# MLP rows written straight to the output, segments' rows added there by DMA: one core of Trainium2, a recurrent attention kernel beside an MLP

## The chip, the cores and the metric

One core of a Trainium2 chip runs the whole kernel. Engines are named as in the profile: PE is TensorE (its weight loads are PEld), DVE is VectorE, ACT is ScalarE, POOL is GpSimd, SP is SyncE. SP and ACT issue DMAs on hardware queues, POOL on the software queue (q0 in the profile). The metric is the device time of one execution in microseconds (us), lower is better. In "the profiled execution" the same program ran under the hardware profiler.

## The reference, cut to what matters

```
xn  = layernorm(x)                                   # 2048 rows of 1024
out = x + A(xn) + B(xn)

B(xn) = gelu(xn @ w1 + b1) @ w2 + b2                 # F = 3584

A(xn): mem = mem0                                    # 8 rows
  for each of 64 segments of 32 rows xs:
      h = concat(mem, xs)                            # 40 rows
      q, k, v = h @ Wq, h @ Wk, h @ Wv               # 32 heads of 128
      p = softmax(mask(q @ k.T / sqrt(128)))
      o = (p @ v) @ Wo
      mem = o[:8]                                    # read by the next segment
      yield o[8:]
```

The segments depend on each other through `mem`; the MLP, B, does not depend on them. The kernel calls `x + B(xn)` of a row its residual, and the output of a row is its residual plus its row of A.

## The kernel before, in words

**First stage, the MLP (to about 417 us).** Rows are tiled by 128, four tiles to a group `tg`, four groups. Each group makes layer norm, transposes, the first product (L468), gelu and the second product (L589; in the last group L622, with b2 and x added by PE at L615 and L616). `keep_xT` writes the transposed rows to DRAM (`hr_d` by segments, `hrL_d` by groups of segments). `keep_R` (L418) writes the residual rows to the DRAM tile `R_n`; those of the last group are issued by ACT. `turn_R` (L455, L457) then copies them with small DMAs from `R_n` into the second halves of `hr_d` and `hrL_d`, in the layout in which the segments' results lie. SP issues these copies for groups 0 and 1, POOL those for group 2, and those of the last group go into a list, `small`, from which POOL issues one or two at each streamed unit in segments 1 to 4.

**Second stage, 64 segments in order.** The weights Wq, Wk, Wv and Wo are cut into 64 units of 512 KB. 46 are resident in SBUF: they are fetched into places that the MLP gives up (`fetch_resident`), and four of them, `LATE`, into a pool `late` that opens after the MLP's pools have closed. The other 18 are streamed in every segment through six slots (`start_stream`, L257 and L259): when PE has used a unit, `unit_done` gives its slot to the next one and SP issues the load. Two of the 18 are kept in PSUM banks and copied from there by DVE (L246). Of one unit of Wo, `PART`, 768 of 2048 columns stay in SBUF, in `half_home`, and the rest (320 KB) is streamed.

A segment's queries, keys and values are made of 24 of its 32 rows and the memory. The 8 rows left over by each of four segments ("left rows") are put together with those of the other three, and their products, made beside those of the segments, serve a group. The order in a segment is: K of the first half of the heads, Q, K of the second half, Q, V, V, then O (`O_UNITS`). In the second K/Q part stand the scores, the exponential `pr` (L860) into the tile `pr_all`, two minima that apply the mask (L867), the sums of the first half (`sums(0)`: products L875 and L881, a logarithm and exponentials on ACT at L886 and L889, DVE's products into `pd_main` and `pd_left` at L896 and L900). The second half follows in the V part, so `pr_all` and `pd_main` are written twice in every segment. `scores(0)` comes after K, Q and K, some 7 us into the segment.

The result of O stands in a PSUM tile `psX`. Three segments of four have their own rows alone in it, 128 partitions by 256 columns; DVE adds the folded half (L1084). The others (`left_o`, 16 of them and the last segment) have 128 by 512, with the left rows of up to four segments, and ACT copies them (L1081). From there PE and DVE put the memory rows into the next segment's transposed input (`put_mem`, L291 and L295). That is the step from segment to segment.

Then DVE adds the residual (L1104). The residual of an ordinary segment lies in `res_home`, half of the tile `hr_home`, and comes with the next x rows in one load of 128 KB (`load_x_rows`, L268; in the first segments two loads of 64 KB by ACT). That of the left rows is loaded into `pr_all` (L1072). POOL then stores the sum with four DMAs (L1137), or, with left rows, first to the DRAM tile `outL_d` (L1109) and from there to the output (L1134). In the last segment SP and ACT store it directly (L1126).

The tiles at the head of SBUF stand at written addresses. `SCRATCH`, 384 bytes of a partition, is for POOL's DMA descriptors, and behind it:

```python
    half_home = nc.alloc_sbuf_tensor_at("half_home", [P, DM], BF16, offset=SCRATCH)
    hr_home = nc.alloc_sbuf_tensor_at("hr_home", [P, 512], BF16, offset=SCRATCH + 2048)
    pd_main = nc.alloc_sbuf_tensor_at("pd_main", [P, 320], BF16, offset=SCRATCH + 3072)

    part_home, pr_all, res_home = half_home[:, 0:PART_COLS], half_home[:, PART_COLS:DM], hr_home[:, 256:512]
```

So in the profile of before `pr_all` appears as `half_home`, and the residual as `hr_home`. [...]

## Time and profile before

| | |
|---|---|
| three runs, us | 1840.64, 1843.55, 1832.82 (median 1840.64) |
| profiled execution, us | 1839.26 |
| its span (first to last instruction), us | 1837.5 |
| granted TensorE clock | 0.996 |
| busy, share of the span | PE 93%, PEld 49%, DVE 52%, ACT 36%, POOL 15% |
| DMA, whole span | 612.94 MB, mean 334 GB/s |
| MLP, segments | to about 417 us, from there to the end |

A busy PE is not PE at its peak: the ends of matmuls are modelled, and short gaps disappear. Waits are put down to the event that came last. Several lines below come from a view of one stretch or one engine in order of time. In a line of the timeline the numbers are start and length in us, and the square bracket tells how long the engine was idle before and what ended that. [...]

### The profile page before, as it was taken

The page shows a single profiled execution, that of the slowest core. Times are in us where ns is not written, and L with a number is a line of the kernel's source. Part 1 is how long each engine was busy: PE and PEld are TensorE (multiplying, and loading weights), DVE is VectorE, ACT ScalarE, POOL GpSimd, SP SyncE. Part 2 cuts the span into 40 slices and gives each one's busy share as a digit, 9 for nine tenths or more (in the row PEclk, how much of TensorE's full clock was granted, in tenths as well). Part 3 has the DMA queues.
Part 4 walks back from the last instruction along what each step waited for, and adds up shares of the span by engine and source line. Part 5 has one row for each costly group of instructions (what it writes and reads, how often), then busy time and mean ns, then how long its engine had stood idle before and what let it go on. Part 6 is the DMA issues. An engine that isn't in the chain of part 4 may idle for free.

```text
span 1837.5 us, 69927 instructions
## 1 busy us (share of the span) xinstructions
PE 1717.9 (93%) x30556; PEld 893.2 (49%) x30576; DVE 955.3 (52%) x2330; ACT 663.8 (36%) x1429; POOL 284.4 (15%) x559
## 2 busy tenths in 40 slices
PE   8999999998999999999999999999999999999997
PEld 4444444444454445454545545454545454545444
DVE  7657483805454545555454555455545454545543
ACT  6334251602333333333333333333333333333333
POOL 0000001501342111111111111112111111111111
PEclk9999999999999999999999999999999999999999
DMA  9931212769999999999999999999999999999998
GB/s 286 313 98 46 55 44 57 260 209 371 397 404 389 391 384 389 381 394 388 373 397 386 400 385 394 374 390 401 389 384 390 383 398 391 397 376 384 389 393 313
DMA packets 229278, 612.94 MB, mean 334 GB/s; under 512 B 46795, under 2 KB 76027, under 8 KB 228972
## 3 DMA queue, kind: packets, MB, share of 16 engines
q1 hardware_dynamic: 207252, 588.05, 84.3%
q0 software_dynamic: 17408, 17.69, 3.0%
q8 instruction: 239, 3.92, 0.8%
q10 hardware_dynamic: 4312, 2.73, 0.5%
q14 instruction: 67, 0.55, 0.1%
HBM read 594.40 MB, written 29.23 MB: 339 GB/s over the span
## 4 chain that ended last, share of the span: by engine, by line
PE 32%; DMA 18%; DVE 4%; ACT 2%; issue 1%; POOL 0%; DVEq 0%; ACTq 0%; SPq 0%
PE acc L739 22%; DMA u<-Wc_K 10%; PE acc L962 6%; DMA outL_d<-half_home 3%; DMA u<-Wc_O 3%; ACT mixed L889 1%; DVE b_oL L804 1%; PE acc L915 1%; DMA hr_home<-hr_d 1%; DVE pd_main L896 1%; PE mixed L848 1%; DMA u<-Wc_V 1%; ACT mixed L886 1%; DMA u<-Wc_Q 0%; PE mixed L854 0%
## 5 line engine op out<-in xcount | busy, mean ns | idle before, releaser
L739 PE MATMUL acc<-u,hr_home 128*32 128x512 bf16 x11520 | 770.8, 380 | 34.0 <-DMA u<-Wc_K 18.2
L739 PEld LDWEIGHTS <-hr_home 128*32 128x32 bf16 x12288 | 342.1, 96 | 317.3 <-issue 57.3
L739 PE MATMUL acc<-u,hrL 128*32 128x512 bf16 x2880 | 248.8, 379 | 3.0 <-DVE folded L978 3.0
L468 PE MATMUL ps<-u 128*128 128x512 bf16 (+1 forms) x920 | 195.7, 375 | 2.0 <-ACT u L388 2.0
L246 DVE TENSOR_SCALAR u<-kept 128x512 uint32<-128x512 uint32 x254 | 163.5, 685 | 35.4 <-PE acc L962 12.3
L962 PE MATMUL acc<-u,d_oL 128*32 128x512 bf16 (+1 forms) x1792 | 153.3, 381 | 11.7 <-DMA u<-Wc_O 9.4
L790 ACT CAST kT<-acc 128x512 bf16<-128x512 f32 x64 | 37.4, 585 | 307.6 <-PE acc L739 307.5
L589 PE MATMUL ps<-u 128*128 128x512 bf16 x657 | 146.2, 379 | 0.8
L962 PEld LDWEIGHTS <-b_oL 128*32 128x32 bf16 (+1 forms) x3381 | 108.4, 98 | 74.5 <-issue 35.9
L896 DVE TENSOR_TENSOR pd_main<-half_home,mixed 128x320 bf16<-128x320 bf16 x128 | 62.4, 487 | 153.2 <-ACT mixed L889 153.2
L468 PEld LDWEIGHTS <-u 128*128 128x128 bf16 x920 | 90.5, 99 | 105.5 <-issue 2.4
L1137 POOL DMA_DIRECT2D out_dram<-hr_home x188 | 96.3, 512 | 294.1 <-DVE hr_home L1104 280.5
L962 PE MATMUL acc<-u,b_oL 128*32 128x256 bf16 (+2 forms) x2062 | 117.1, 289 | 20.2 <-DMA u<-Wc_O 19.5
L804 DVE STREAM_TRANSPOSE b_oL<-b_oL 128x512 bf16<-128x512 bf16 x128 | 90.6, 708 | 64.8 <-ACT b_oL L790 64.8
L268 POOL DMA_DIRECT2D hr_home<-hr_d x58 | 32.8, 565 | 581.3 <-PE acc L739 576.1
L962 PEld LDWEIGHTS <-d_oL 128*32 128x32 bf16 (+1 forms) x2048 | 70.3, 99 | 84.7 <-issue 28.0
L739 PEld LDWEIGHTS <-hrL 128*32 128x32 bf16 x3072 | 82.9, 96 | 51.2 <-issue 7.7
L790 ACT CAST b_oL<-acc 128x512 bf16<-128x512 f32 x128 | 75.1, 587 | 86.1 <-PE acc L739 86.1
L589 PEld LDWEIGHTS <-u 128*128 128x128 bf16 x672 | 65.3, 98 | 77.3 <-DVE g_u L550 0.4
L889 ACT ACTIVATE mixed<-mixed,small_consts 128x160 f32<-128x160 f32 x256 | 94.2, 368 | 8.4
L542 ACT ACTIVATE g_xb<-ps,b1col 128x512 bf16<-128x512 f32 x112 | 76.8, 686 | 55.5 <-PE ps L468 54.7
L794 ACT CAST v<-acc 128x512 bf16<-128x512 f32 x128 | 75.1, 587 | 48.9 <-PE acc L739 48.6
(129 smaller groups left out, 2011.6 us busy)
## 6 DMA issues: line engine op xcount, KB each, us to landing
u<-Wc_K SPq DMA_DIRECT2D x320, 512.0 KB
u<-Wc_V SPq DMA_DIRECT2D x256, 512.0 KB
u<-Wc_O SPq DMA_DIRECT2D x256, 512.0 KB
u<-Wc_Q SPq DMA_DIRECT2D x128, 512.0 KB
u<-Wc_O SPq DMA_DIRECT2D x64, 320.0 KB
u<-in_B_w_dram SPq DMA_DIRECT2D x28, 512.0 KB
hr_home<-hr_d POOLq DMA_DIRECT2D x58, 128.0 KB, 5.5
u<-in_A_Wq_dram SPq DMA_DIRECT2D x14, 512.0 KB
```

The costliest lines, as they stand in the source:

```text
L246: nc.vector.tensor_single_scalar(out=out, in_=in_, scalar=0, op=ALU.bitwise_or)
L468: nc.tensor.matmul(ps[:, SEG * s0:SEG * s1].rearrange("p (s t) -> p s t", t=SEG), lhsT=w1_sb[fb // 2][:, kt, (fb % 2) * P:(fb % 2 + 1) * P ...
L542: nc.scalar.activation(out=xb[:, :], in_=ps[:, :], func=ACT.Identity, bias=b1col[:, fb:fb + 1], scale=1.0)
L589: nc.tensor.matmul(ps[:, :], lhsT=gts[fc // 4][:, fc % 4, t * P:(t + 1) * P], rhs=w2_sb[fc // 2][:, fc % 2, cs], start=(fc == 0), stop=(fc ...
L739: nc.tensor.matmul(o, lhsT=lhs[:, i, :], rhs=m, start=(i == seq[0]), stop=(i == seq[-1]), tile_position=(0, 32 * j),)
L790: cp(out=out, in_=ps.rearrange("p (h e) -> p h e", e=32))
L794: cp(out=t[:, :], in_=ps[:, :])
L804: nc.vector.transpose(out=home, in_=home)
L889: nc.scalar.activation(out=mixed[:, 160 * b:160 * b + 160], in_=mixed[:, 0:160], func=ACT.Exp, scale=-1.0, bias=off[:, b:b + 1],)
L896: nc.vector.tensor_tensor(out=pdA.rearrange("p c b q -> p b c q"), in0=prA[:, None, :, :].to_broadcast([P, 2, 4, 40]), in1=dd, op=ALU.mult,)
L962: nc.tensor.matmul(acc[r0:r0 + rows, c:c + wide], lhsT=lhs[:, 4 * (i % 4) + 2 * u + k, :], rhs=cols, start=start, stop=stop, tile_position ...
L1137: nc.gpsimd.dma_start(out=out_flat[rows, 256 * j:256 * j + 256], in_=res[32 * j:32 * j + NX, :])
```

## The change

`keep_R` writes the residual rows into the output itself. `R_n`, `outL_d`, `turn_R`, the list `small`, all loads of residuals and DVE's L1104 go. At the end of a segment the sum of A stands in `pr_all` (256 columns), with left rows also in `pd_main`; `put_mem` reads it there, and POOL issues DMAs that add it to the output's rows (`accum_op`): four for an ordinary segment, eight with left rows, in the last segment too. `hr_d` and `hrL_d` hold only x rows, so a load is 64 KB, and POOL issues it in all segments. `half_home` keeps 1024 columns of `PART`, and 256 KB of it are streamed; `pr_all` is a tile of its own, where half of `hr_home` was. The MLP's pool of small tiles `ma` is closed ahead of the last group's second product, and `late` is opened there with the four LATE units fetched at once; the first two places of the queue `late_units` are now those of `xt2` and `xt3`.

```diff
-    hr_d = dram.tile([NSEG + 1, P, 512], BF16, name="hr_d")
-    hrL_d = dram.tile([NGRP + 1, P, 512], BF16, name="hrL_d")
-    R_n = dram.tile([S, DM], BF16, name="R_n")
-    outL_d = dram.tile([NGRP, 2 * SEG, DM], BF16, name="outL_d")
+    hr_d = dram.tile([NSEG, P, 256], BF16, name="hr_d")
+    hrL_d = dram.tile([NGRP, P, 256], BF16, name="hrL_d")
...
-    hr_home = nc.alloc_sbuf_tensor_at("hr_home", [P, 512], BF16, offset=SCRATCH + 2048)
+    hr_home = nc.alloc_sbuf_tensor_at("hr_home", [P, 256], BF16, offset=SCRATCH + 2048)
+    pr_all = nc.alloc_sbuf_tensor_at("pr_all", [P, 256], BF16, offset=SCRATCH + 2560)
...
         elif unit == PART:
-            nc.sync.dma_start(out=t[:, PART_COLS:], in_=copies[unit])
+            nc.sync.dma_start(out=t[:, DM:], in_=copies[unit])
...
     def load_x_rows(s, eng=nc.sync):
-        n = 512 if s > 5 else 256
-        eng.dma_start(out=hr_home[:, 0:n], in_=hr_d[s, :, 0:n])
-        nxt["hT"] = hr_home[:, 0:256].rearrange("p (k t) -> p k t", k=KT)
+        eng.dma_start(out=hr_home[:, :], in_=hr_d[s, :, :])
+        nxt["hT"] = hr_home.rearrange("p (k t) -> p k t", k=KT)
...
             eng = nc.scalar if ttg >= NT - 4 else nc.sync
-            eng.dma_start(out=R_n[ttg * P:ttg * P + P, :], in_=rsb[:, :])
+            eng.dma_start(out=out_flat[ttg * P:ttg * P + P, :], in_=rsb[:, :])
...
-                for t in range(4):
-                    turn_R(4 * tg + t, nc.gpsimd if tg == 2 else nc.sync)
...
+                mlp.close()
+                late = ctx.enter_context(tc.tile_pool(name="late", bufs=1))
+                for unit in LATE:
+                    res_tiles[unit] = late.tile([P, 2048], BF16, name="W_" + "_".join(map(str, unit)))[:, :]
+                    fetch(res_tiles[unit], unit)
                 for fc in range(FC):
...
-        late_units = deque(lambda unit=unit: fetch_late(unit) for unit in LATE)
-        late_units += [lambda: fetch_resident("xt2"), lambda: fetch_resident("xt3")]
+        late_units = deque([lambda: fetch_resident("xt2"), lambda: fetch_resident("xt3")])
...
-            if 1 <= s <= 4:
-                turn_R(NT - 5 + s, nc.gpsimd, small)
...
-                load_x_rows(s + 1, nc.scalar if s < 5 else nc.gpsimd)
+                load_x_rows(s + 1, nc.gpsimd)
...
+            o_tiles = [pr_all[:, :], pd_main[:, 0:256]] if left_o else [pr_all[:, :]]
+            if left_o:
+                nc.scalar.copy(out=o_tiles[0], in_=psX[:, 0:256])
+                nc.vector.tensor_copy(out=o_tiles[1], in_=psX[:, 256:512])
+            else:
+                nc.vector.tensor_tensor(out=o_tiles[0], in0=psX[:, 0:256], in1=st["folded"][:, :], op=ALU.add)
+            let_go(psX)
...
-                nc.vector.tensor_tensor(out=r_rows, in0=o, in1=r_rows, op=ALU.add)
...
+            def add_out(o, r):
+                nc.gpsimd.dma_start(out=o, in_=r, accum_op=ALU.add)
+
+            for w, r in enumerate(o_tiles):
+                if not left_o:
+                    for j in range(4):
+                        add_out(out_flat[rows, 256 * j:256 * j + 256], r[32 * j:32 * j + NX, :])
+                    continue
+                s0 = GRP * og - 2
+                segs = [i for i in range(max(s0, 0), s + 1)]
+                for b in range(2):
+                    cs = slice(256 * (2 * b + w), 256 * (2 * b + w) + 256)
+                    add_out(out_flat[rows, cs], r[64 * b + m0:64 * b + m0 + NX, :])
+                    p0 = 64 * b + NL * (segs[0] - s0)
+                    add_out(
+                        out_flat.rearrange("(s r) c -> s r c", r=SEG)[segs[0]:segs[-1] + 1, NX:SEG, cs],
+                        r[p0:p0 + NL * len(segs), :],
+                    )
```

More of the change, by code (lines that the diff above doesn't have):

```diff
@@ L57 @@
 AT_BANKS, AT_PART = 5, 4
-PART_COLS = 768
 def pass_order():
@@ L140 @@
     half_home = nc.alloc_sbuf_tensor_at("half_home", [P, DM], BF16, offset=SCRATCH)
-    hr_home = nc.alloc_sbuf_tensor_at("hr_home", [P, 512], BF16, offset=SCRATCH + 2048)
+    hr_home = nc.alloc_sbuf_tensor_at("hr_home", [P, 256], BF16, offset=SCRATCH + 2048)
+    pr_all = nc.alloc_sbuf_tensor_at("pr_all", [P, 256], BF16, offset=SCRATCH + 2560)
     pd_main = nc.alloc_sbuf_tensor_at("pd_main", [P, 320], BF16, offset=SCRATCH + 3072)
-    part_home, pr_all, res_home = half_home[:, 0:PART_COLS], half_home[:, PART_COLS:DM], hr_home[:, 256:512]
     slabs = ctx.enter_context(tc.tile_pool(name="slabs", bufs=1))
@@ L161 @@
     qL = [consts.tile([P, 16, SEG], BF16, name="qL"), qL_last]
-    ident = res_home[:, 0:P]
+    ident = pr_all[:, 0:P]
     make_identity(nc, ident)
@@ L212 @@
     copies = {
-        unit: dram.tile([P, 2048 - PART_COLS if unit == PART else 2048], BF16, name="Wc_" + "_".join(map(str, unit)))[:, :]
+        unit: dram.tile([P, DM if unit == PART else 2048], BF16, name="Wc_" + "_".join(map(str, unit)))[:, :]
         for unit in reversed(ORDER) if IS_STREAMED[unit] and unit not in KEPT
@@ L220, in fetch @@
             h = 4 * i + 2 * u
-            nc.sync.dma_start(out=t[:, 0:DM - PART_COLS], in_=Wo_v[:, h, PART_COLS:])
-            nc.sync.dma_start(out=t[:, DM - PART_COLS:], in_=Wo_v[:, h + 1, :])
+            nc.sync.dma_start(out=t, in_=Wo_v[:, h + 1, :])
         elif w == "O":
@@ L266, in load_x_rows @@
     def load_x_rows(s, eng=nc.sync):
-        n = 512 if s > 5 else 256
-        eng.dma_start(out=hr_home[:, 0:n], in_=hr_d[s, :, 0:n])
-        nxt["hT"] = hr_home[:, 0:256].rearrange("p (k t) -> p k t", k=KT)
+        eng.dma_start(out=hr_home[:, :], in_=hr_d[s, :, :])
+        nxt["hT"] = hr_home.rearrange("p (k t) -> p k t", k=KT)
     def load_left_rows(g, eng=nc.sync):
         hr = hrp.tile([P, 256], BF16, name="hrL")
-        eng.dma_start(out=hr[:, :], in_=hrL_d[g, :, 0:256])
+        eng.dma_start(out=hr[:, :], in_=hrL_d[g, :, :])
         nxt["hL"] = hr.rearrange("p (k t) -> p k t", k=KT)
@@ L282, with put_mem @@
     nat_home, q_home = outs[0][:, :, 32:64], outs[1][:, :, 24:64]
-    def put_mem(o_sb, hT, ps, nb=4):
+    def put_mem(o_at, hT, ps, nb=4):
         nc_ = KT // nb
@@ L291, in put_mem @@
                 nc.tensor.matmul(
-                    psM[32 * q:32 * q + 32, c, :, :], lhsT=o_sb[:, 4 * c + q, :], rhs=rows,
+                    psM[32 * q:32 * q + 32, c, :, :], lhsT=o_at[4 * c + q], rhs=rows,
                     start=(c == 0), stop=True, skip_group_check=True, tile_position=(0, 32 * q),
@@ L301 @@
     NT = S // P
-    with tc.tile_pool(name="ma", bufs=2) as ma, tc.tile_pool(name="mps", bufs=6, space=PSUM) as mps:
+    mlp = ctx.enter_context(ExitStack())
+    with tc.tile_pool(name="mps", bufs=6, space=PSUM) as mps:
+        ma = mlp.enter_context(tc.tile_pool(name="ma", bufs=2))
         eps_t = ma.tile([P, 1], F32, name="eps_t", bufs=1)
@@ L411, in keep_xT @@
                 nc.sync.dma_start(
-                    out=hrL_d[4 * tg + 2 * k:4 * tg + 2 * k + 2, :, 0:256].rearrange("g p c -> p g c"),
+                    out=hrL_d[4 * tg + 2 * k:4 * tg + 2 * k + 2, :, :].rearrange("g p c -> p g c"),
                     in_=xl[k][:, :, :, :, :].rearrange("p g k i t -> p g (k i t)"),
@@ L417, in keep_R @@
             eng = nc.scalar if ttg >= NT - 4 else nc.sync
-            eng.dma_start(out=R_n[ttg * P:ttg * P + P, :], in_=rsb[:, :])
+            eng.dma_start(out=out_flat[ttg * P:ttg * P + P, :], in_=rsb[:, :])
         def main_row(slot):
             return NL * slot + NL
-        def with_left(seg):
-            return seg % GRP == 1 or seg == NSEG - 1
-        def turn_R(ttg, eng, small=None):
-            for i in range(4):
-                seg = 4 * ttg + i
-                rows = R_n[seg * SEG:(seg + 1) * SEG, :].rearrange("t (j c) -> t j c", j=4)
-                og, slot = divmod(seg + 2, GRP)
-                both = [
-                    t[:, 256:512].rearrange("(h r) c -> r h c", h=2)
-                    for t in (hr_d[min(4 * og + 1, NSEG - 1) + 1, :, :], hrL_d[og, :, :])
-                ]
-                halves = [rows.rearrange("t (h w) c -> t w h c", w=2)[:, w, :, :] for w in range(2)]
-                if with_left(seg):
-                    m0 = main_row(slot)
-                    pairs = [(both[w][m0:m0 + SEG, :, :], halves[w]) for w in range(2)]
-                else:
-                    pairs = [(hr_d[seg + 1, :, 256:512].rearrange("(j t) c -> t j c", j=4), rows)]
-                rows_at = [NL * slot]
-                if seg < 2:
-                    rows_at.append(NL * (slot ^ 2))
-                elif seg >= NSEG - 2:
-                    rows_at.append(main_row(1) + SEG + NL * slot)
-                for r0 in rows_at:
-                    pairs += [(both[w][r0:r0 + NL, :, :], halves[w][NX:SEG, :, :]) for w in range(2)]
-                for o, r in pairs:
-                    if small is None:
-                        eng.dma_start(out=o, in_=r)
-                    else:
-                        small.append(lambda o=o, r=r: nc.gpsimd.dma_start(out=o, in_=r))
         def new_xnT(tg):
@@ L608 @@
                 start_stream("xn3")
-                put_mem(o_sb, nxt["hT"], mps.tile([P, 512], F32, name="ps"))
+                put_mem([o_sb[:, n, :] for n in range(8)], nxt["hT"], mps.tile([P, 512], F32, name="ps"))
                 nc.sync.dma_start(out=d_oL[:, :], in_=Wo_v[:, h + 1, :])
@@ L638 @@
                     keep_R(4 * tg + t, xtoks[4 * tg + t])
-    with tc.tile_pool(name="late", bufs=1) as late, \
-            tc.tile_pool(name="banks", bufs=1, space=PSUM) as banks:
+    with tc.tile_pool(name="banks", bufs=1, space=PSUM) as banks:
         nc.scalar.preload_act_table_set("natural_log_exp_and_others")
-        small = deque()
         free_banks = deque(f"acc{k}" for k in range(3))
@@ L689, in unit_tile @@
             return res_tiles[unit]
-        def fetch_late(unit):
-            t = late.tile([P, 2048], BF16, name="W_" + "_".join(map(str, unit)))[:, :]
-            res_tiles[unit] = t
-            fetch(t, unit)
-        late_units = deque(lambda unit=unit: fetch_late(unit) for unit in LATE)
-        late_units += [lambda: fetch_resident("xt2"), lambda: fetch_resident("xt3")]
+        late_units = deque([lambda: fetch_resident("xt2"), lambda: fetch_resident("xt3")])
         def unit_done(unit):
@@ L704, in unit_done @@
                     late_units.popleft()()
-                for _ in range(2 if len(small) > 8 else 1):
-                    if small:
-                        small.popleft()()
         O_UNITS = ORDER[48:]
@@ L932, in o_columns @@
             def o_columns(unit, t, k, blocks):
-                homes = [part_home if unit == PART and DM * k + 256 * b < PART_COLS else t for b in blocks]
+                homes = [half_home if unit == PART and k == 0 else t for b in blocks]
                 if len(blocks) == 2 and homes[0] is homes[1]:
@@ L984 @@
                 keep(IN_BANKS, 0, half_home[:, :], 3)
-                nc.sync.dma_start(out=part_home, in_=Wo_v[:, 4 * PART[1] + 2 * PART[2], 0:PART_COLS])
+                nc.sync.dma_start(out=half_home[:, :], in_=Wo_v[:, 4 * PART[1] + 2 * PART[2], :])
                 copy_bits(mixed[:, 468:512].bitcast(U32), mask.bitcast(U32))
@@ L1034 @@
                 at[1] = [lambda: values(0, (0, 1))]
-            def load_res():
-                st["res"] = res_home
-                if s < 5:
-                    nc.scalar.dma_start(out=res_home, in_=hr_d[s + 1, :, 256:512])
             psV1, psV1L = half_pass("V", 1, left_v[1], at)
@@ L1045 @@
             if not final:
-                load_x_rows(s + 1, nc.scalar if s < 5 else nc.gpsimd)
-            else:
-                nc.gpsimd.dma_start(out=res_home, in_=hr_d[s + 1, :, 256:512])
+                load_x_rows(s + 1, nc.gpsimd)
             if first:
@@ L1058 @@
                 at[9] = [lambda: left_values(1, psV1L)]
-            at.setdefault(0, []).append(load_res)
             psX = new_acc()
@@ L1069 @@
                     fn()
-                if n == 1 and left_o:
-                    st["resL"] = pr_all
-                    (nc.scalar if s < 5 else nc.gpsimd).dma_start(
-                        out=st["resL"][:, :], in_=hrL_d[og, :, 256:512]
-                    )
-            nw = 2 if left_o else 1
-            if not final:
-                o_sb = nat_home
-                no = 16 if left_o else 8
-                o = psX[:, 0:32 * no].rearrange("p (h e) -> p h e", e=32)
-                if left_o:
-                    nc.scalar.copy(out=o_sb[:, 0:no, :], in_=o)
-                else:
-                    folded = st["folded"].rearrange("p (h e) -> p h e", e=32)
-                    nc.vector.tensor_tensor(out=o_sb[:, 0:no, :], in0=o, in1=folded, op=ALU.add)
+            o_tiles = [pr_all[:, :], pd_main[:, 0:256]] if left_o else [pr_all[:, :]]
[5 more added lines that the diff above has]
+            let_go(psX)
+            if not final:
                 ahead = []
@@ L1092 @@
                     lead_products(LEAD // 2)
-                put_mem(o_sb, nxt["hT"], mixed[:, 224:288], 4 // nw)
+                o_at = [o[:, 32 * n:32 * n + 32] for o in o_tiles for n in range(8)]
+                put_mem(o_at, nxt["hT"], mixed[:, 224:288], 4 // len(o_tiles))
                 if led:
                     lead_products(LEAD)
-            res, rows = st["res"], slice(s * SEG, s * SEG + NX)
-            tiles = (res, st["resL"]) if left_o else (res,)
-            for w, r in reversed(list(enumerate(tiles))):
-                if left_o:
-                    o = psX[:, 256 * w:256 * w + 256].rearrange("p (h e) -> p h e", e=32)
-                else:
-                    o = o_sb[:, 0:8, :]
-                r_rows = r.rearrange("p (h e) -> p h e", e=32)
-                nc.vector.tensor_tensor(out=r_rows, in0=o, in1=r_rows, op=ALU.add)
-                if left_o and not final:
-                    for b in range(2):
-                        c0 = 256 * (2 * b + w)
-                        nc.gpsimd.dma_start(out=outL_d[og, :, c0:c0 + 256], in_=r[64 * b:64 * b + 64, :])
@@ L1110 @@
-            let_go(psX)
-            left_rows = [
-                (sl, (GRP * og - 2 + sl) * SEG + NX) for sl in range(GRP) if s - GRP < GRP * og - 2 + sl <= s
-            ]
-            left_rows = [(sl, row) for sl, row in left_rows if row >= 0]
-            if final:
-                engines = [nc.sync, nc.scalar]
-                n = 0
-                for w, r in enumerate(tiles):
-                    for b in range(2):
-                        cs = slice(256 * (2 * b + w), 256 * (2 * b + w) + 256)
-                        pieces = [(rows, slice(64 * b + m0, 64 * b + m0 + NX))]
-                        for sl, row in left_rows:
-                            p0 = 64 * b + NL * sl
-                            pieces.append((slice(row, row + NL), slice(p0, p0 + NL)))
-                        for o, i in pieces:
-                            engines[n % 2].dma_start(out=out_flat[o, cs], in_=r[i, :])
-                            n += 1
-            elif left_o:
-                pairs = [(out_flat[rows, :], outL_d[og, m0:m0 + NX, :])]
-                pairs += [
-                    (out_flat[row:row + NL, :], outL_d[og, NL * sl:NL * sl + NL, :]) for sl, row in left_rows
-                ]
-                for o, r in pairs:
-                    small.append(lambda o=o, r=r: nc.gpsimd.dma_start(out=o, in_=r))
-            else:
-                for j in range(4):
-                    nc.gpsimd.dma_start(out=out_flat[rows, 256 * j:256 * j + 256], in_=res[32 * j:32 * j + NX, :])
@@ new lines @@
+            rows = slice(s * SEG, s * SEG + NX)
+            def add_out(o, r):
[15 more added lines that the diff above has]
+                    )
@@ L1138 @@
             if not final:
                 hT = nxt["hT"]
-        while small:
-            small.popleft()()
 _INS = ['A_x', 'A_mem0', 'A_Wq', 'A_Wk', 'A_Wv', 'A_Wo', 'A_seg_len', 'B_x', 'B_w1', 'B_b1', 'B_w2', 'B_b2']
```

## The prediction

> **What bounds the kernel now.** I read the busy table by stretches first, with granted clock and DMA share, because the page's averages mix the MLP (to 417 us) with the 64 segments behind it. The columns are stretch, length, busy time of PE, PEld, DVE, ACT and POOL, clock, DMA share, GB/s.

> ```profile
> 417.00:460.00 43.00, 38.48 (x816) 21.23 (x820) 24.19 (x53) 11.96 (x27) 5.29 (x10) 1.00 1.03 385
> 460.00:560.00 100.00, 91.93 (x1974) 49.88 (x1966) 49.06 (x119) 35.40 (x83) 40.11 (x74) 1.00 1.03 400
> 560.00:1834.00 1274.00, 1179.30 (x25809) 632.40 (x25805) 645.03 (x1559) 454.90 (x1057) 198.57 (x380) 1.00 1.00 387
> ```

> All DMA engines are busy all the time from 417 us to the end, while PE has 7% idle. Next came TensorE's waits from 460 us on (total, times, longest), then the page's DMA queues:

> ```profile
> PE acc L962 <- DMA u<-Wc_O: 28.2, 60, 1.3
> PE acc L739 <- DMA u<-Wc_K: 18.0, 33, 1.9
> PE mixed L848 <- DVE b_oL L804: 12.2, 44, 0.4
> ```
> ```profile
> q1 hardware_dynamic: 207252, 588.05, 84.3%
> q0 software_dynamic: 17408, 17.69, 3.0%
> ```

> With two rows too small to show, PE waits 47.7 us in 62.5 segments for streamed weights, 0.76 us in each. So the loop is **bound by DMA**, and PE comes close behind: a segment takes 21.9 us (the group of four repeats every 87.7 us in the chain of waits, 826.57 to 1790.84 us in 11 groups), and PE could do it in about 21.9 - 0.76 = 21.15. The prices of a byte follow from the queues: q1, 0.843 x 1837.5 / 588.05 = 2.63 us of all engines per MB; q0 (POOL's), 0.030 x 1837.5 / 17.69 = 3.12 us per MB.

> The third reading is of the timelines around a segment's end. An ordinary one, then one that carries the left rows too:

> ```profile
> 845.63 0.42 DVE L1084 TENSOR_TENSOR d_oL<-acc,folded 128x256 bf16<-128x256 f32 x1 [1.44 <-PE acc L962]
> 846.54 0.28 DVE L1104 TENSOR_TENSOR hr_home<-d_oL,hr_home 128x256 bf16<-128x256 bf16 x1
> 847.12 2.21 POOL L1137 DMA_DIRECT2D out_dram<-hr_home  x4 [7.30 <-DVE hr_home L1104]
> 853.59 0.36 ACT L860 ACTIVATE half_home<-mixed 128x224 bf16<-128x224 f32 x1
> ```
> ```profile
> 826.00 1.12 POOL L1109 DMA_DIRECT2D outL_d<-half_home  x2 [7.55 <-DVE hr_home L1104]
> 832.24 0.36 ACT L860 ACTIVATE half_home<-mixed 128x224 bf16<-128x224 f32 x1 [0.74 <-DMA outL_d<-half_home]
> 833.25 0.25 PE L875 MATMUL mixed<-half_home,small_consts 128*32 128x160 bf16 x4 [0.47 <-DVE mixed L246]
> ```

> In the ordinary one the exponential (L860) waits for no DMA. In the other its tile is still being read by stores, it starts 0.74 us late, and PE stands 0.47 us. The change puts every segment in that position.

> [...] I price an add at twice a store. [...] L1137's rows last 0.51 us, their landing takes 5.1 us.

> **The change, part by part** (DMA time in the loop, all engines).

> Removed:
> - The half unit: each segment streams 256 KB of PART and not 320: 64 x 65,536 B = 4.19 MB x 2.63 = **11.0 us**.
> - Residuals beside the x rows: 58 loads of 128 KB become 64 KB, 3.80 MB x 3.12 = **11.9 us**; five separate ones (0.33 MB), 1.0 us.
> - Residuals of left rows, 17 x 64 KB = 1.11 MB: 3.5 us.
> - Left rows through outL_d: 64 stores of 32 KB (2.10 MB, 6.5 us), then 62 x 16 + 16 x 48 KB to the output (1.80 MB, 5.6 us); L1137's 188 x 12 KB (2.31 MB, 7.2 us).
> - turn_R in segments 1 to 4: half of POOL's copies from R_n, 1.33 MB, 4.1 us. Its other three quarters run during the MLP, where PE is 98 to 100% busy by itself (stretches from 20 to 417 us); they are worth nothing, on SP's queue or on POOL's.
> - The four LATE units, 2.10 MB, 5.5 us, are fetched at about 366 us, once the bias products are issued and the small tiles free. SP's fetches of w2 and gT places stand behind them there. That is hidden: the DMAs move 170 to 260 GB/s from 360 to 420 us, so 2 MB fit. But in segment 0 SP now meets xt2's and xt3's fetches, which wait for the stores of rows (issued by ACT from 416.4 us), some 4 us early, with streams behind them. I count 3 of the 5.5.

> Sum, as counted: 53.8 us. Added: the adds write each output byte once, 4.19 MB: 13.1 us at a store's price, **26.2 at twice**, 39.3 at three times. Net 40.7, **27.6** or 14.5 us.

> Not all arrives. PE's waits for weights are 0.76 us a segment and the steady saving of (27.6 - 7.1) / 64 = 0.32 us leaves PE about 0.4 of slack, so waits of its own begin to show: I take three quarters, **21 us**. Bounds: half (PE takes over) and all.

> The new wait. After an ordinary segment pr_all holds the result, read by four adds; the next segment's first exponential writes pr_all. Over 43 ordinary segments from the sixth on, read in the timelines and counted from L1084's end: the first store is issued at 1.24 us (median), the fourth lands at 8.13, the exponential starts at 7.68 (quartiles 7.36 and 7.77). The adds need no L1104: POOL starts about 0.3 us after L1084, so four adds at a store's speed land at 8.13 - 1.24 + 0.3 = **7.2 us**, 0.5 us in time. An add may land later by some d: not below zero[...]; above, the longest landings of POOL's stores and loads are 7.0 and 7.1 us (L1109, L268) against medians of 5.1 to 5.6, so d of 2 is not excluded. I take d = 0.5: POOL's copies from HBM to HBM (L1134)[...] land after 5.3 us, its stores after 5.1[...]; then, pair by pair over the 43 segments, the exponential waits 0.26 us on average, with 0.15 on PE (0.27 less than ACT's, as 0.74 against 0.47). That is inside the 0.4 us of slack: **nothing**, while DMA remains the bound. What stands behind the exponential on ACT are its logarithm and the V copies; for it wait DVE's minima and PE's sums.

> With left rows: pr_all's four adds land some 0.4 us sooner than the stores of L1109, for L1104 is gone and the copy is of 256 columns, but four more adds from pd_main follow, issued to about 4.2 us, landed by 9.3 + d, where L896 writes pd_main at about 9.4 to 10. Between a gain of 0.4 us and a loss of 1.5 us, 16 times: I take nothing. Descriptors of eight adds could also fill POOL's ring; I leave up to 2 us x 16 in the range for that.

> DVE loses 64 adds, ACT and DVE split one copy of 0.58 us, PE loses 17 weight loads and as many products by wider blocks: all beside a bound DMA, nothing.

> The end. Now PE ends at 1831.08 and the span at 1837.5, 6.4 us, with ten stores from two hardware queues. Then: a copy of 0.4 us, 0.3 to POOL, eight adds at 0.55, a landing: SP and ACT issue to 1834.7 and the span ends 2.8 us later, so 0.4 + 0.3 + 4.4 + 2.8 = 7.9: **+1.5 us**.

> Sum: 1839.3 (the profiled execution) - 21 + 1.5 = 1820; the median of the runs stands 1.4 us above that execution, so **1821 us**. Changes under 0.5% (9 us) can't be told from none here.

> **The rivals.**
> - *The adds are as cheap as stores and PE keeps up*: 1839.3 - 40.7 x 0.9 + 1.5 + 1.4 = 1806. For: small transfers on q0 cost little more per byte than q1's. [...] 0.10.
> - *No change*: adds cost three times a store or more, or PE's own chain takes over: 14.5 x 0.5 - 1.5 = 6 us gained, 1835. For: PE is 93% busy. Also here: the edit moves traffic that was hidden. Against that, DMA is never idle in the loop. 0.16.
> - *Slower: the adds land late and the exponential waits.* Place: ACT's first L860 of each segment. With d = 1.5 us, by the same pairs, it waits 1.0 us on average and PE 0.75, all of the 0.76, so the gain is gone; this is the point of decision, a landing of 6.7 us. With d = 2, PE stands 1.19 us: a period of 21.15 + 1.19 = 22.34, 0.44 us over now, x 64 = 28, less 5 of early savings, plus 1.5: 1865. For: the margin of 0.5 us is smaller than the spread of the landings (the fourth lands from 7.3 to 9.5). Against: of the 16 segments whose stores already stand in the way, 12 wait, 10.9 us in all, though there the stores start 1.36 us after the copy and not 0.3. 0.24.

> **How the numbers follow.** The forecast has 0.50, with 1812 to 1830. With the cheap adds that makes faster 0.60; same 0.16; slower 0.24. The range from 1803 to 1862 takes in the cheap case and most of the slow one; it leaves out under a tenth below and about a tenth above.

> **What would show it.** Right: q0 from 17.7 MB to under 13 [...]; POOL's adds at 0.5 to 0.6 us each and landing in 5 to 6; waits of the exponential for adds below 20 us in total; a group of four in about 86.4 us; the DMA share still 1.00. Wrong: landings of adds at 7 us, ACT's waits for them of 60 us or more with PE's L875 behind; or a DMA share clearly under 1.00 with PE at the same waits, which would mean that PE's chain was the bound; or adds' packets at several times a store's price.

## The result, and the profile after

The changed kernel takes **2059.17 us** (median of six runs, 2048.32 to 2069.12); the kernel before took 1839.36 in the same comparison. The ratio is 1.1192, 95% interval 1.1136 to 1.1249: 12% slower, where 1821 us were forecast and 1803 to 1862 given as the range. The profiled execution took 2069.12 us, its span is 2067.4.

The page's DMA queues come first (packets, MB, share of 16 engines). In the lines below L1036 is the adds, L811 the exponential, L818 the minima, L826 the first product of the sums and L847 the write of `pd_main`.

```profile
q1 hardware_dynamic: 200492, 581.16, 76.6%
q0 software_dynamic: 24128, 8.48, 3.0%
```

The bytes went as planned: 7 MB less by the hardware queue, 9 MB less by POOL's. But the share of the hardware queue fell from 84.3 to 76.6%. DMA is no longer what the loop waits for, as the windows show (length, busy PE, PEld, DVE, ACT, POOL, clock, DMA share, GB/s; the second one lies behind a segment with left rows):

```profile
1000.00:1500.00 500.00, 423.25 (x8916) 216.42 (x8907) 218.12 (x516) 155.77 (x360) 93.64 (x117) 0.94 0.91 331
```
```profile
1099.00:1113.00 14.00, 8.31 (x140) 3.79 (x144) 4.38 (x13) 4.29 (x11) 2.71 (x3) 0.62 0.44 123
```

The waits from 460 us on (total, times, longest) name what took its place:

```profile
POOL out_dram L1036 <- issue: 369.5, 121, 6.4
...
DVE pr_all L818 <- ACT pr_all L811: 203.8, 90, 9.0
ACT pr_all L811 <- DMA out_dram<-pr_all: 163.6, 47, 8.7
...
PE mixed L826 <- DVE mixed L242: 106.0, 15, 7.6
...
DVE pd_main L847 <- DMA out_dram<-pd_main: 96.5, 16, 7.4
```

The exponential waits for adds (163.6 us), DVE's minimum behind it, and PE for both; PE's row names a short DVE copy (L242) because that comes right behind the two minima: in the stand shown below the minima end at 1099.86 us, the copy starts at 1099.89 and takes 0.23, and PE starts at 1100.17. Fifteen waits of PE make 106 us, 7 us each: about one in each group of four segments. The waits are put in place by the time from one segment's result to the next, a median for each of the four places in a group, before and after: **behind the result with left rows 21.0 and 33.2 us**, then 22.1 and 23.2, then 20.7 and 21.9, and up to the next result with left rows 23.8 and 23.8. Times 16 that is 195 us in one place and some 36 in two others.

In the timeline, POOL in an ordinary segment and then behind left rows, with ACT and PE beside it:

```profile
1061.75 3.30 POOL L1036 DMA_DIRECT2D out_dram<-pr_all  x4 [4.74 <-DVE pr_all L1018]
```
```profile
1085.12 1.78 POOL L1036 DMA_DIRECT2D out_dram<-pr_all  x2 [7.46 <-ACT pr_all L1015]
1090.16 0.85 POOL L1036 DMA_DIRECT2D out_dram<-pr_all  x1 [3.26 <-issue]
1091.59 0.93 POOL L1036 DMA_DIRECT2D out_dram<-pr_all  x1 [0.58 <-issue]
1096.47 0.80 POOL L1036 DMA_DIRECT2D out_dram<-pd_main  x1 [3.94 <-issue]
1099.29 1.77 POOL L1036 DMA_DIRECT2D out_dram<-pd_main  x2 [2.02 <-issue]
1102.13 0.94 POOL L1036 DMA_DIRECT2D out_dram<-pd_main  x1 [1.07 <-issue]
```
```profile
1099.17 0.36 ACT L811 ACTIVATE pr_all<-mixed 128x224 bf16<-128x224 f32 x1 [7.23 <-DMA out_dram<-pr_all]
```
```profile
1100.17 0.33 PE L826 MATMUL mixed<-pr_all,small_consts 128*32 128x160 bf16 x4 [6.90 <-DVE mixed L242]
```

Four adds go out in one stretch. Of eight, two go out, and then POOL stands ("issue") before most of the others: the last is out 18 us after the first. Nothing that the profile names holds it. The experiments were made to find what does.

### The profile page after: what moved, and what is told of

The parts are those of the page before. It is cut to its first block, busy times and chain, and to the rows that moved or that the text cites. A ratio compares the mean times of both kernels' runs of the same rounds, so it can differ in the third digit from the quotient of the medians.

```text
span 2067.4 us, 69575 instructions
## 1 busy us (share of the span) xinstructions
PE 1778.2 (86%) x30539; PEld 889.3 (43%) x30559; DVE 940.8 (46%) x2266; ACT 666.0 (32%) x1430; POOL 324.7 (16%) x432
## 3 DMA queue, kind: packets, MB, share of 16 engines
q1 hardware_dynamic: 200492, 581.16, 76.6%
q0 software_dynamic: 24128, 8.48, 3.0%
## 4 chain that ended last, share of the span: by engine, by line
PE 49%; DMA 23%; issue 13%; POOL 7%; DVE 4%; ACT 3%; ACTq 0%; POOLq 0%; DVEq 0%; SPq 0%
PE acc L690 15%; PE acc L913 11%; DMA out_dram<-pr_all 9%; PE ps L430 9%; POOL out_dram L1036 7%; PE ps L551 7%; DMA u<-Wc_K 5%; DMA out_dram<-pd_main 3%; DMA u<-Wc_V 3%; DMA u<-Wc_Q 2%; PE acc L866 2%; PE ps L587 2%; DVE b_oL L755 1%; DVE pd_main L847 1%; ACT mixed L840 1%
## 5 line engine op out<-in xcount | busy, mean ns | idle before, releaser
L690 PE MATMUL acc<-u,hr_home 128*32 128x512 bf16 x11520 | 817.1, 399 | 36.9 <-DMA u<-Wc_K 25.3
L1036 POOL DMA_DIRECT2D out_dram<-pr_all x256 | 215.8, 1169 | 459.4 <-issue 266.6
L242 DVE TENSOR_SCALAR u<-kept 128x512 uint32<-128x512 uint32 x254 | 163.4, 685 | 49.6 <-PE acc L690 27.6
L847 DVE TENSOR_TENSOR pd_main<-pr_all,mixed 128x320 bf16<-128x320 bf16 x128 | 62.4, 488 | 231.3 <-ACT mixed L840 134.7
L826 PE MATMUL mixed<-pr_all,small_consts 128*32 128x160 bf16 x512 | 34.7, 259 | 146.0 <-DVE mixed L242 106.0
L913 PE MATMUL acc<-u,d_oL 128*32 128x512 bf16 (+1 forms) x1792 | 159.3, 399 | 0.5 <-issue 0.2
L430 PEld LDWEIGHTS <-u 128*128 128x128 bf16 x920 | 90.6, 99 | 105.4 <-issue 2.4
L818 DVE TENSOR_TENSOR pr_all<-pr_all,mixed 128x96 bf16<-128x96 bf16 (+1 forms) x256 | 38.1, 190 | 210.5 <-ACT pr_all L811 210.1
L811 ACT ACTIVATE pr_all<-mixed 128x224 bf16<-128x224 f32 x128 | 45.8, 358 | 247.7 <-DMA out_dram<-pr_all 165.4
L913 PE MATMUL acc<-u,b_oL 128*32 128x256 bf16 (+1 forms) x1998 | 114.4, 290 | 6.0 <-DMA u<-Wc_O 5.5
L690 PEld LDWEIGHTS <-hrL 128*32 128x32 bf16 x3072 | 77.5, 96 | 54.8 <-PE acc L913 6.9
```

The costliest lines, as they stand in the source:

```text
L242: nc.vector.tensor_single_scalar(out=out, in_=in_, scalar=0, op=ALU.bitwise_or)
L430: nc.tensor.matmul(ps[:, SEG * s0:SEG * s1].rearrange("p (s t) -> p s t", t=SEG), lhsT=w1_sb[fb // 2][:, kt, (fb % 2) * P:(fb % 2 + 1) * P ...
L690: nc.tensor.matmul(o, lhsT=lhs[:, i, :], rhs=m, start=(i == seq[0]), stop=(i == seq[-1]), tile_position=(0, 32 * j),)
L811: nc.scalar.activation(out=pr, in_=mixed[:, 0:224], func=ACT.Exp, scale=INV_SQRT_DH)
L847: nc.vector.tensor_tensor(out=pdA.rearrange("p c b q -> p b c q"), in0=prA[:, None, :, :].to_broadcast([P, 2, 4, 40]), in1=dd, op=ALU.mult,)
L913: nc.tensor.matmul(acc[r0:r0 + rows, c:c + wide], lhsT=lhs[:, 4 * (i % 4) + 2 * u + k, :], rhs=cols, start=start, stop=stop, tile_position ...
```

## The experiments

Two theories stood at the start. **Full ring**: the 384 B a partition that the kernel sets aside for POOL's DMAs (`SCRATCH`, here called the ring) have no room for eight adds, and POOL stands until an earlier one has landed. **Slow adds**: adding itself is slow, or collides on its rows of HBM, and the tiles are held for that reason. In the trace POOL's issues behind left rows stand at 0.4, 1.1, 6.1, 7.5, 13.0, 14.7, 15.7 and 17.6 us after the copy (medians of 17), and the landings of the first six at 5.8, 7.2, 12.7, 14.4, 15.3 and 17.3: from the third on, each issue follows the landing of the add two places ahead by about 0.3 us.

### A larger ring

```diff
-SCRATCH = 384
-SMALL = 3712
+SCRATCH = 896
+SMALL = 3200
```
(To make room, the half unit goes back to 768 resident columns, with `pr_all` beside them.)

> The changed kernel with 896 B of a partition for POOL's descriptors in place of 384; the 512 B come from half_home, which keeps 768 columns of PART as before did (320 KB streamed). Theory 'full ring': with left rows eight adds do not fit among POOL's descriptors, POOL stands until earlier adds have landed, and pr_all and pd_main stay taken; with room for all the segment after left rows falls from 33.2 us to about 23 and the kernel takes about 1890 us. Rival 'slow adds': the adds land late because reading and writing the output is slow in itself; more room changes nothing and the kernel stays above 2000 us.

Measured: 1943.16 us, ratio 1.0544 (1.0490 to 1.0598). POOL's timeline behind left rows (`pr_all` is part of `half_home` here):

```profile
1027.95 3.60 POOL L1038 DMA_DIRECT2D out_dram<-half_home  x4 [7.73 <-ACT half_home L1017]
1030.47 1.90 POOL L1038 DMA_DIRECT2D out_dram<-pd_main  x1
1034.64 1.76 POOL L1038 DMA_DIRECT2D out_dram<-pd_main  x2 [2.26 <-issue]
...
```

Five go out in one stretch where two did, and the segment behind left rows falls from 33.2 to 25.2 us. Slow adds alone can't do that, for the adds are the same. The size was missed: I had expected all eight to fit.

### Stores in place of adds

The stores overwrite the MLP's rows, so that part of the output is missing.

```diff
-                nc.gpsimd.dma_start(out=o, in_=r, accum_op=ALU.add)
+                nc.gpsimd.dma_start(out=o, in_=r)
```

> The changed kernel with the same DMAs to the same rows as plain stores: the residual rows are overwritten and not added to (that part of the output is left out). Theory 'full ring': [...] eight of them fit, POOL does not stand, about 1830 us; the stores land in about 5 us. Rival 'slow adds': also about 1830[...]. Rival 'shape of the DMAs'[...]: stays above 1950.

Measured: 1927.94 us, ratio 1.0438 (1.0396 to 1.0481). POOL behind left rows:

```profile
1030.53 0.51 POOL L1036 DMA_DIRECT2D out_dram<-pr_all  x1 [7.38 <-ACT pr_all L1015]
1031.27 1.15 POOL L1036 DMA_DIRECT2D out_dram<-pr_all  x2 [0.23 <-issue]
1036.29 0.63 POOL L1036 DMA_DIRECT2D out_dram<-pr_all  x1 [3.87 <-issue]
1036.91 1.28 POOL L1036 DMA_DIRECT2D out_dram<-pd_main  x2
...
```

The forecast of 1830 fell, and usefully: plain stores stand too, only later (the fourth, not the third). So the stand isn't made by adding alone. That the stores get one DMA further fits a ring in which an add takes more room than a store.

### No adds at all

```diff
-                nc.gpsimd.dma_start(out=o, in_=r, accum_op=ALU.add)
+                return
```

> The changed kernel without the DMAs at a segment's end: A's part of the output is left out. It shows what the removed loads, copies and stores, the half unit kept whole and the early late pool are worth without what was put in their place. By the prediction's sums (53.8 us of DMA time removed, three quarters of it arriving) about 1800 us; if TensorE's own chain is the bound, 1825 or more.

A's part of the output is left out here. Measured: 1809.02 us, ratio 0.9804 (0.9765 to 0.9843), with all DMA engines busy at 383 GB/s (share 1.00, 1000 to 1500 us). What the change takes away is worth 36 us (0.0196 of 1843). So the loss lies in what it puts in.

### Left rows by way of DRAM

```diff
+                if not final:
+                    for b in range(2):
+                        cs = slice(256 * (2 * b + w), 256 * (2 * b + w) + 256)
+                        nc.gpsimd.dma_start(out=outL_d[og, :, cs], in_=r[64 * b:64 * b + 64, :])
+                    continue
...
+                add_out(out_flat[rows, :], outL_d[og, m0:m0 + NX, :], max_dma_last_dim=4096)
+                add_out(
+                    out_flat.rearrange("(s r) c -> s r c", r=SEG)[segs[0]:segs[-1] + 1, NX:SEG, :],
+                    outL_d[og, p0:p0 + NL * len(segs), :].rearrange("(s r) c -> s r c", r=NL), max_dma_last_dim=4096,
+                )
```

> The changed kernel, but left rows go through outL_d as in before: four stores of 64x256, and once they have landed two adds from there to the output (24 rows, and all left rows, in pieces of 2048 elements). Ordinary segments as in the changed kernel. Theory 'full ring': no POOL stand at issue, the segment after left rows back to about 21 to 22 us, ordinary ones 1.1 us longer than before, about 1870 us in all. Rival 'slow adds' in ordinary segments carries most of the loss: above 1950.

Measured: 1883.56 us, ratio 1.020 (1.0158 to 1.0241), 14 us above the expectation. The segment behind left rows is back at 21.1 us. What remains is the wait of ordinary segments, in two lines of the waits:

```profile
ACT pr_all L812 <- DMA out_dram<-pr_all: 54.5, 37, 2.4
...
PE mixed L827 <- DVE pr_all L819: 42.0, 37, 2.0
```

### The result in another tile

As the last kernel, and:

```diff
-            o_tiles = [pr_all[:, :], pd_main[:, 0:256]] if left_o else [pr_all[:, :]]
+            o_tiles = [pr_all[:, :], pd_main[:, 0:256]] if left_o else [pd_main[:, 0:256]]
```

> As e4_bounce, and the result of an ordinary segment stands in pd_main, which the next segment writes some 2.5 us later than pr_all. Theory (ring plus late adds plus the price of an add): the exponential no longer waits for an add in any segment, the +1.1 us of the two ordinary positions goes, and what is left over the 1809 us of e3_noadd is the DMA time of the adds and of the stores to DRAM: about 1850 us, DMA share 1.00. Rival (the adds slow everything by contention on the DMA engines, the exponential's wait is only where it shows): no gain over e4_bounce, 1880 us.

Measured: 1834.7 us, ratio **0.9951** (0.9934 to 0.9969): faster than the kernel before, and 15 us under what I expected. No wait of ACT or DVE for an add is left among the waits. The move of one tile is worth 46 us (by the ratios, give or take 8; the two profiled executions lie 38.7 us apart). Windows of the last kernel and then of this one:

```profile
1000.00:1500.00 500.00, 457.28 (x9960) 240.31 (x9953) 243.54 (x579) 175.20 (x409) 90.40 (x123) 1.00 0.99 374
```
```profile
1000.00:1500.00 500.00, 464.35 (x10256) 250.76 (x10248) 250.44 (x596) 178.82 (x419) 94.26 (x127) 0.99 1.01 382
```

With the wait the DMA share still reads 0.99, yet only 374 GB/s are moved and not 382. A share near 1.00 did not say that DMA hides a wait.

### Half of the eight adds, one half and then the other

First without the adds of left rows, then without those of the segment's own rows:

```diff
-                    add_out(
-                        out_flat.rearrange("(s r) c -> s r c", r=SEG)[segs[0]:segs[-1] + 1, NX:SEG, cs],
-                        r[p0:p0 + NL * len(segs), :],
-                    )
```
```diff
-                    add_out(out_flat[rows, cs], r[64 * b + m0:64 * b + m0 + NX, :])
```

> The changed kernel without the adds of left rows (4x8x256); those rows of the output stay without A. Theory [...] POOL issues them as in an ordinary segment (about 0.4, 1, 1.6 and 2.2 us after the copy) and does not stand; the segment after the left rows falls from 33.2 to 22 to 23.5 us; in all about 1875 us. Rival (the adds of the left rows are not to blame, the two tiles being held is): 30 us there, about 2010 us.

> The changed kernel without the adds of a segment's own rows in the segments that carry left rows; those rows stay without A there. As many adds as in e6_main_only, 64 KB of data instead of 48. Theory [...] each waits for the landing of the one before: issues at about 0.4, 6, 12 and 18 us after the copy, the segment after the left rows still takes 30 to 35 us, in all 2000 to 2070 us although half of the adds are gone. Rival (the ring is counted in DMAs or in bytes): as e6_main_only, below 1900 us.

Measured: 1859.69 us (expected 1875; ratio 1.0080, 1.0054 to 1.0107) without the left rows, **2057.34** (1.1145, 1.1087 to 1.1204) with them alone: taking away four of eight adds brought 200 us in one case and nothing in the other. POOL behind a segment with left rows, first kernel, then second:

```profile
1101.01 1.64 POOL L1036 DMA_DIRECT2D out_dram<-pr_all  x2 [7.26 <-ACT pr_all L1015]
1102.07 2.22 POOL L1036 DMA_DIRECT2D out_dram<-pd_main  x2
```
```profile
1077.96 0.94 POOL L1036 DMA_DIRECT2D out_dram<-pr_all  x1 [7.48 <-ACT pr_all L1015]
1083.91 0.95 POOL L1036 DMA_DIRECT2D out_dram<-pr_all  x1 [5.01 <-issue]
1090.71 0.89 POOL L1036 DMA_DIRECT2D out_dram<-pd_main  x1 [5.85 <-issue]
1093.52 0.88 POOL L1036 DMA_DIRECT2D out_dram<-pd_main  x1 [1.92 <-issue]
```

Four adds of 24x256 go out without a stop; four of 4x8x256 go out one by one, each about 0.3 us after the landing of the one before (medians of 17). It is neither the number of adds nor their bytes (48 and 64 KB) that counts, but their shape. The queue lines of the two kernels' pages show a difference:

```profile
q0 software_dynamic: 14336, 7.38, 2.5%
```
```profile
q0 software_dynamic: 20864, 7.64, 2.4%
```

The changed kernel has 24128 packets there and 68 adds of each kind more than one of the two, so an add of left rows has (24128 - 14336) / 68 = 144 packets, one of 24x256 (24128 - 20864) / 68 = 48. By size, in the trace, these are 32 pieces of 512 B (the whole 16 KB), 96 of 8 B and 16 ends of 4 B, against 24 (the whole 12 KB), 8 and 16.

By packets the stands of the adds fall in order. With 384 B, 48 + 144 = 192 went out at once, and so did four adds of 24x256 (192); a third add behind the first two (240) stood, and so did a second of 4x8x256 (288). With 896 B five adds (432) went out and a sixth (576) stood. From these runs I estimate the ring's room at 192 to 240 packets of adds with 384 B and at 432 to 576 with 896. The count does not carry over to stores. A load of x rows has 32 packets in the trace, so that in the page of the kernel with stores, whose q0 has 12416, the 324 stores have (12416 - 64 x 32) / 324 = 32 each on average; there three (96) went out and the fourth (128) stood, while the four stores of an ordinary segment go out without a stop (at 1007.81 us, in 2.13 us). The runs thus bound the ring for adds. What in a DMA's shape takes the room was not shown.

### Parts of the change alone

The early pool in the kernel before:

```diff
...
+                mlp.close()
+                late = ctx.enter_context(tc.tile_pool(name="late", bufs=1))
+                for unit in LATE:
+                    res_tiles[unit] = late.tile([P, 2048], BF16, name="W_" + "_".join(map(str, unit)))[:, :]
+                    fetch(res_tiles[unit], unit)
...
```

> The kernel before with one part of the change alone: the MLP's pool of small tiles closed early and the four LATE units fetched there. The prediction counts 3 to 5.5 us of DMA time in the first segment, three quarters of it arriving: 1837 to 1841 us beside 1843, not to be told from no change. Rival (the fetches come in the way of w2 and of the first segment's streams): 1845 us or more.

Measured: 1839.14 us, ratio 0.9983 (0.9964 to 1.0002), some 3 us, not to be told from none.

The half unit as before, in the kernel without adds:

```diff
...
-            nc.sync.dma_start(out=t[:, DM:], in_=copies[unit])
+            nc.sync.dma_start(out=t[:, PART_COLS:], in_=copies[unit])
...
```

> As e3_noadd (no DMA brings A's results to the output; A left out of it), with the half unit as before: 768 of its columns stay, 320 KB of it are streamed in each segment and not 256. The prediction counts 11.0 us of DMA time for the difference, three quarters arriving, 8 us: about 1817 us beside the 1809 of e3_noadd. Rival (PE is the bound once the output's DMAs are gone, so the bytes cost nothing): 1809 us; the other end, all of it arriving: 1820 us.

Measured: 1821.77 us, ratio 0.9884 (0.9851 to 0.9917), against 0.9804: keeping the half unit whole is worth 13 to 15 us (by medians and by ratios). The two kernels were not timed side by side, and the intervals of their ratios leave some 9 us on either side, so that this can't be told from the 11.0 us of its bytes, or from three quarters of them.

### The price of adding

Two more kernels on the base of the one with results in `pd_main`. In the first, ordinary results too go to DRAM and are added from there in pieces of 3 KB, in the middle of the next segment, and the adds of left rows wait until then as well; in the second plain copies stand in place of the adds, so that the output lacks x and B.

```diff
-                        add_out(out_flat[rows, 256 * j:256 * j + 256], r[32 * j:32 * j + NX, :])
+                        nc.gpsimd.dma_start(out=mid_d[s, :, 256 * j:256 * j + 256], in_=r[32 * j:32 * j + NX, :])
+                    later.append(lambda o=out_flat[rows, :], i=mid_d[s, :, :]: add_out(o, i, max_dma_last_dim=4096))
```
```diff
-                nc.gpsimd.dma_start(out=o, in_=r, accum_op=ALU.add, **kw)
+                nc.gpsimd.dma_start(out=o, in_=r, **kw)
```

> As e5_bounce_pd, and ordinary results too are first stored to DRAM (four stores) and added from there to the output by one DMA with pieces of 3 KB, issued in the middle of the next segment, so that POOL waits for no store. In e4_bounce's trace an added packet of 3,072 B took 252 ns, 5.1 us per MB for all engines, against 9.1 for the added packets of 512 B; stores cost 2.9. For the 2.26 MB of ordinary rows: 8.0 in place of 20.6 us per 2.26 MB would be 5.1 x 2.26 + 2.9 x 2.26 = 18.1 against 20.6: 2 to 3 us faster than e5_bounce_pd, about 1832 us. Rival (what is left is the number of DMAs and packets, not their length): 1840 us or more.

> e5_bounce_pd with plain copies in place of its adds, so that the MLP's rows are overwritten: the output lacks x and B. Same DMAs, bytes written, rings and waits; what is taken away is the adding. By packets: (9.1 - 2.9) us per MB for 2.26 MB of 512-B pieces, 14 us, and (5.1 - 2.7) for 1.9 MB of long ones, 4.5 us; three quarters arrive: 1821 us beside 1834.7. Rival (adding costs an extra latency, not DMA time): within 4 us of e5_bounce_pd.

Measured: 1839.24 us, ratio 0.9962 (0.9939 to 0.9985), the same as with direct adds (0.9951) within the intervals, so the small gain was not seen; and 1821.98 us, 0.9888 (0.9852 to 0.9923), as expected: adding costs 12 us, give or take 7 by the intervals. In the packets of the kernel with the second tile, an added packet of 512 B took 66.6 ns (mean, 460 to 1800 us); in the one with copies the stores of the same rows, which go two rows to a packet of 1,024 B, took 46.9, so that the add takes 2.8 times as long for a byte. Packets of 3,072 B took 256.2 and 124.8 ns, 2.1 times. (In the expectation "8.0 in place of 20.6" is a slip; the sum it compares is 18.1 against 20.6.)

### The end

On the same base, the last segment without adds: its MLP rows are loaded early, DVE adds, two hardware queues store.

```diff
...
+            if final:
+                for w, r in enumerate(last):
+                    nc.vector.tensor_tensor(out=r, in0=psX[:, 256 * w:256 * w + 256], in1=r, op=ALU.add)
+                for n, (o, i) in enumerate(last_pieces):
+                    (nc.sync, nc.scalar)[n % 2].dma_start(out=o, in_=i)
...
```

> As e5_bounce_pd, but in the last segment no DMA adds: its MLP rows are loaded beside the O products into a place of Wq that is no longer needed, DVE adds them, and SP and ACT store the twelve pieces on two hardware queues, as the kernel before did. Theory (the ring also sets the end: in the trace of e5_bounce_pd 13.6 us lie between PE's end and the span's end, 14.0 in the changed kernel, where the prediction had 7.9): the tail falls to 6.4 us as before, so 7 us faster than e5_bounce_pd, about 1827.5 us and a ratio of 0.991 to before. Rival (the tail is the landing of the last stores whatever their queue): no more than 2 us gained.

Measured: **1826.88 us, ratio 0.9911** (0.9880 to 0.9943), the fastest version that makes the whole output: 0.9% under the kernel before. The last eight adds of the changed kernel, and this kernel's end:

```profile
2054.22 1.77 POOL L1036 DMA_DIRECT2D out_dram<-pr_all  x2 [19.86 <-ACT pr_all L1015]
...
2063.75 0.93 POOL L1036 DMA_DIRECT2D out_dram<-pd_main  x1 [1.20 <-issue]
```
```profile
1822.16 0.76 DVE L1029 TENSOR_TENSOR u<-acc,u 128x256 bf16<-128x256 f32 x2 [3.92 <-DMA u<-out_dram]
1822.61 2.19 SPq L1031 DMA_DIRECT2D out_dram<-u  x6
1822.62 2.52 ACTq L1031 DMA_DIRECT2D out_dram<-u  x6
```

PE ends at 2053.4 us with 14.0 to go in the one, at 1822.1 with 5.2 to go in the other. The step from 0.9951 to 0.9911 is 7 us, with intervals that leave as much on either side; the 8 us between the tails, 13.6 to 5.2, are in the traces.

## Why the prediction was wrong

The ratios form a ladder from the kernel before to the changed one, each rung times 1843 us. The kernels of the rows at 0.9804 and 0.9888 leave a part of the output out.

| step | ratio | us | the prediction |
|---|---|---|---|
| before | 1 | | |
| all parts removed, no output | 0.9804 | -36 | three quarters of 53.8: -40 |
| output copied, left rows by DRAM, second tile | 0.9888 | +15 | with the next row: three quarters of 26.2, +20 |
| copies become adds | 0.9951 | +12 | (in the row above) |
| ordinary results in `pr_all` | 1.0200 | +46 | nothing |
| left rows added directly | 1.1192 | +183 | nothing, 32 at most |

- **The left rows**, "I take nothing" and "up to 2 us x 16 in the range": the step that failed most. The ring was seen and mis-sized: some 11.4 us x 16. The prediction had the last of eight adds issued by about 4.2 us; it was issued at 17.6. The room that the eight adds take was not counted. In packets of the changed kernel's trace they ask for 4 x (48 + 144) = 768, where 192 went out at once and 240 did not, so that six of eight wait for a landing. The landings come 5.4 to 6.8 us after the issue for the first four and 2.2 to 2.5 for the next three, when the loop and its streams stand too. The trace of before does not give that count, but it had the sign: POOL stands at the copies of `turn_R` in the first segments, 33.2 us in 15 waits before the copies to `hr_d` alone, also marked "issue". After the four stores of an ordinary result:

```profile
451.53 2.07 POOL L1137 DMA_DIRECT2D out_dram<-hr_home  x4 [7.12 <-DVE hr_home L1104]
453.70 0.57 POOL L457 DMA_DIRECT2D hr_d<-R_n  x1
456.49 0.58 POOL L457 DMA_DIRECT2D hr_d<-R_n  x1 [2.22 <-issue]
```

The four stores and the first copy go out without a stop; the second copy is issued 0.3 us after the first store has landed. Only 2.9 us of other engines' waits are put down to these copies there, and the prediction did not use the sign.
- **The ordinary wait**: two sizes failed. d was taken as 0.5 us, an estimate; the fourth add lands 8.8 us after the result (median), not 7.2, so d is 1.6. In the trace of the changed kernel the exponential waits 41.3 us over the 43 segments, 0.96 each: the 1.0 of the slow rival at d = 1.5. That landing, 8.8 - 2.2 = 6.6 us from the issue, is just its point of decision, 6.7. But the rival's price fell short as well. A wait inside "the 0.4 us of slack: nothing" was the wrong step. With the second tile PE waits 61.1 us for weights in all, with the wait (left rows by way of DRAM, results in `pr_all`) 51.8: of PE's 42.0 us at L827 only 9 came out of those, and the run grew by 46, the trace by 38.7. A stand of PE is not paid from its later waits for weights here. That the slots come free later meanwhile and the transfers behind them start later is likely, as fewer GB/s are moved (374 against 382); it was not tried by itself.
- **The price of an add**, twice a store's, was my assumption, which no row of before showed: right for long packets (256.2 against 124.8 ns), short for packets of 512 B (2.8 times for a byte). In sum, 27 us for output and adding against 20: a small miss, and the 27 include the way of the left rows by DRAM and the longer end, which the 20 do not.
- **What is removed**: right. The half unit gave 13 to 15 where 11.0 of DMA time were counted, the LATE units about 3 where three were (the intervals fix neither to better than several us). The DMA share stays at 1.00 or more behind 560 us in the versions without adds and in that with the second tile, which fits the reading of the bound.
- **The end**, +1.5 us: 14.0 - 6.4 = +7.6 in the trace, for the eight adds meet the same ring, and a landing after the last one is issued. In the kernel that took the adds away there the tail is 5.2.
- **The signs**: POOL's bytes under 13 MB came (8.48). Four adds of an ordinary segment start 0.53 us apart, as foreseen. "Waits of 60 us or more with PE behind", named as the sign of a wrong forecast, came with 163.6. A group of four takes 102.1 us, not 86.4. The DMA share fell to 0.91 from 1000 to 1500 us because the loop stood, not for the reason that the prediction gave for such a fall.

## What to carry to other kernels

Before DMAs are moved to POOL's queue, look at their shape and not at their number and bytes alone: here an add of 4x8x256 had 144 packets and one of 24x256 had 48, and with 384 B adds of 192 packets went out at once and of 240 did not. Past that, POOL stood for whole landings (5.4 to 6.8 us for the first four), and what waited for its tiles stood with it. Look in the trace for such stands ("issue") first. A tile that a DMA still reads is best one that nobody writes soon: moving one result by one tile was worth 46 us. And a DMA share of 0.99 did not prove that a new wait was hidden: compare the GB/s, here 374 and 382.
